# A Fourier mixer with a gated feed-forward net: the eight PSUM banks shared out anew between transforms and first layer

## The chip, the cores and the metric

One core of one Trainium2 chip runs the whole program. The metric is device time in microseconds (us) of one execution, the median of several runs. TensorE (PE in the profile; PEld is its weight load) does the matrix products into PSUM, which has eight banks of 512 fp32 columns on 128 partitions. ScalarE (ACT) and VectorE (DVE) read PSUM and free its banks; GpSimd (POOL) and SyncE (SP) issue most DMAs here.

## The reference

```python
X = np.fft.rfft(x, axis=1)                  # x: 8 x 3008 x 256
Yr = Xr @ w_r - Xi @ w_i + b_r
Yi = Xr @ w_i + Xi @ w_r + b_i
Y = soft_threshold(Yr, 0.01) + 1j * soft_threshold(Yi, 0.01)
y = np.fft.irfft(Y, n=3008, axis=1)         # then 24064 tokens of 256
gate = 1 / (1 + np.exp(-(y @ w_gate)))      # 256 -> 1536
out = (gate * (y @ w_val)) @ w_out          # 1536 -> 256
```

The feed-forward weights arrive as 64-bit floats and are turned on the chip into pairs of fp32r words (high and low part); a product of two such pairs is three matmuls.

## The kernel before

**The transform.** A sequence of 3008 = 47 x 64 is transformed in two steps. Step A of a sequence (`fwd_a`, eight units) multiplies by the 47-point table `fa_sb`; step B (`fwd_b`) does the 64-point part, `mix` (or `mix4` for the first sequence) multiplies by `w_r` and `w_i`, `inv_b` goes back by 64 points, and `inv_a` (units again) goes back by 47 points. Between the steps the data goes through HBM: `zd` after step A, `vd` after `inv_b`, and `yd` for the finished tokens that the last stage uses.

A unit of step A holds two row halves of an input tile (`j`, partitions 0 to 46 and 64 to 110) and two column groups (`c`). `products_a` takes two PSUM tiles `pa[0]` and `pa[1]`, one for each `j`, and issues four 47x64x512 fp32 products, which use four different quarters of the array; each is two records in the trace. Then the two banks are copied out, by ACT and DVE or by ACT alone (L191). `halves_a` does the same for the third and fourth sequences with tiles `xfh` loaded in halves and results in `azh` tiles of tag `st`, of which there are `NST` = 3; `inv_b` puts its result `vz` (L327) into the same tag.

**The banks.** Pool `psf` has `FFT_BANKS` = 3 banks, shared by all transform tiles: `pa` (2 for a unit), `pb` (1, freed by the copy `xsf`, L264), `pm` and `pm3` (2 for a mix, freed by DVE, L288 to L293), `pi` (1, freed by the copy `vz`), `pia` (2 for a unit of `inv_a`). Pool `psl` has `L1_BANKS` = 3 banks for the first layer (`pg` and `pv` of `ffn1`) and `L2_BANKS` = 2 for the second (`po` of `ffn2`). When the transforms are done, `psf` is closed and `psg` opened in its place.

**The stages.**
1. Sequence 0 and half of sequence 1 go through step A, then sequence 0 through B, mix and back. The first feed-forward weights are converted beside it (`ops`, `start_part`). The order is written by hand (`tc.manual_schedule`).
2. Twelve `ffn` units (token chunk 0, one for each of the 12 slices of 128 hidden columns), also by hand: `ffn1` for a slice, then `ffn2` for the slice two before, then one or two `halves_a` units. The conversion of the remaining weights is woven into `ffn1` by `hook`.
3. The other 96 `ffn` units, with the other sequences' transforms spread between them by weights (`rates`). Here the framework's planner orders the instructions of each engine: by the order of the program where its own model finds the operands and a free bank, otherwise something later goes first.
4. The remaining 19 pairs of 512-token blocks, without transforms: `half` forms seven products for each 2 x 2 block of the first layer in four banks (`open_banks`: `pa1`, `pb1`, `pc1` from `psl`, `pd1` from `psg`), with `second` between them, by hand.

In the page, L189 is the product of step A, L191 its copies, L251 `fwd_b`, L286 `mix`, L308 `mix4`, L323 to L325 `inv_b`, L359 `inv_a`, L423 to L425 `ffn1`, L429 the sigmoid that frees `pg`, L431 the multiplication that frees `pv`, L451 to L453 `ffn2`, L658 to L660 `second`, L683 the products of stage 4, L810 to L818 the conversion, L861 matmuls on zeros or weights that keep TensorE busy.

Of the kernel before, what the change touches and what calls it, by code (L numbers as in the profile page):

```python
# [9 lines left out]
F32 = mybir.dt.float32  # L10
# [9 lines left out]
R2, R1 = 47, 64  # L20
# [4 lines left out]
CW = 512  # L25
NPL = 9
HW = 512
FFT_BANKS, L1_BANKS, L2_BANKS = 3, 3, 2

NF2K, NR2K, NLD, NST, NBIG, NMF, NME, NVF, NVO, NHH, NSG, NYF = 5, 4, 3, 3, 5, 3, 2, 2, 1, 3, 2, 3  # L30
NCB, NTMP, NHP = 10, 9, 12


# [73 lines left out]
def tile_fft_mix_ffn(ctx: ExitStack, tc, x, w_r, w_i, b_r, b_i, w_one, w_out, mf, mi, mis, fa, fb, out):  # L107
    nc = tc.nc

    B, D, S = x.shape[0], w_r.shape[0], R1 * R2  # L110
    P = 128
# [19 lines left out]
    fft = ExitStack()  # L131
    cw = fft.enter_context(tc.tile_pool(name="cw", bufs=1))
    p2 = fft.enter_context(tc.tile_pool(name="p2", bufs=2))
    psl = ctx.enter_context(tc.tile_pool(name="psl", bufs=3, space=bass.MemoryType.PSUM))
    psfs = ExitStack()
    psf = psfs.enter_context(tc.tile_pool(name="psf", bufs=FFT_BANKS, space=bass.MemoryType.PSUM))

    def bank(name, tag="fft", bufs=FFT_BANKS):
        return (psf if tag == "fft" else psl).tile([P, 512], F32, tag=tag, bufs=bufs, name=name)
# [8 lines left out]
    fa_sb = cw.tile([P, P], F32, name="fa_sb")[:, :64]  # L148
# [32 lines left out]
        move(nc.sync, xf, xv[b, h])  # L181
        held["x", b, h] = xf

    def products_a(xs, outs, copies):
        pa = [bank("pa") for _ in range(2)]
        for j in range(2):
            rows = slice(64 * j, 64 * j + R2)
            for c in range(2):
                nc.tensor.matmul(pa[j][64 * c:64 * c + 64], fa_sb[rows], xs[c][rows], start=True, stop=True)  # L189
        for copy, o, t in zip(copies, outs, pa):  # L190
            copy(o, t.rearrange("p (h c) -> p h c", h=2))  # L191

    def fwd_a(b, h):

        xf = held["x", b, h]
        at = xf[:, 0:2], xf[:, 2:4]
        products_a(at, at, (nc.scalar.copy, nc.vector.tensor_copy if b < 2 else nc.scalar.copy))

    def store_a(b, h, queue=nc.sync):
        move(queue, held.pop(("x", b, h)), zv[b][h], True)  # L200
# [6 lines left out]
    def halves_a(b, u):  # L207

        xs = [held.pop(("xh", b, 2 * u + c)) for c in range(2)]
        az = [p2.tile([P, 2, D], F32, tag="st", bufs=NST, name="azh") for _ in range(2)]  # L210
        products_a(xs, az, (nc.scalar.copy, nc.scalar.copy))
        for j in range(2):
            move(nc.gpsimd, az[j], zv[b][u, :, :, 2 * j:2 * j + 2], True)
# [179 lines left out]
    outs = {}  # L393
# [70 lines left out]
    def fft_units(bs, ms):  # L464
# [5 lines left out]
        def step_a(i):  # L470
            if i == 0:
                for k in range(min(PRE, len(aa))):
                    load_a(*aa[k])
            if i + PRE < len(aa):
                load_a(*aa[i + PRE])
            fwd_a(*aa[i])
            store_a(*aa[i])
# [103 lines left out]
    xs = {}  # L581
# [90 lines left out]
    banks = {}  # L672
# [12 lines left out]
        return product  # L685

    def open_banks(k):
        banks[k] = [bank(t, "l1", L1_BANKS)[:, :HW] for t in ("pa1", "pb1", "pc1")] + [
            psg.tile([P, 512], F32, tag="l1d", bufs=1, name="pd1")[:, :HW]]

    def half(k, extra):

# [3 lines left out]
        if k not in banks:  # L696
            open_banks(k)
            early = False
        else:
            early = True  # L700
# [188 lines left out]
    with tc.manual_schedule():  # L889
# [3 lines left out]
        for h in range(na):  # L893
            fwd_a(0, h)
            store_a(0, h)
            if h in (1, 3, 4):
                load_a(1, {1: 1, 3: 2, 4: 3}[h])
            if h == 2:
                load_mix()
# [7 lines left out]
        for h in range(EARLY):  # L907
            fwd_a(1, h)
            if h == 1:
                wi_sb = mix_weights()  # L910
# [109 lines left out]
    for j in range(NF, len(ffn)):  # L1020
        c, f = divmod(j, NF)
# [4 lines left out]
        while side and (acc >= side[0][0] or j >= (part if len(side) > n_last else end) - 1):  # L1026
# [12 lines left out]
            if not side:  # L1039
                psfs.close()  # L1040
                psg = ctx.enter_context(tc.tile_pool(name="psg", bufs=1, space=bass.MemoryType.PSUM, reuse_waits="tile"))
# [15 lines left out]


    open_banks(0)
    first_product = products(0)  # L1060
    a, b, c, d = banks[0]
# [62 lines left out]
```

## Time and profile before

| | us |
|---|---|
| median of 3 runs | 2793.51 |
| lowest, highest | 2792.45, 2795.2 |
| the profiled execution | 2796.54 |
| its span | 2794.7 |
| TensorE busy in the span | 2764.7 (99%) |
| VectorE busy | 2041.3 (73%) |
| ScalarE busy | 1362.3 (49%) |
| GpSimd busy | 726.4 (26%) |

TensorE's busy time counts a matmul until its modelled end: the second layer's 512-column matmuls stand with 0.39 us each, while one starts 0.23 us after the other. So busy time hides short waits, and the starts of the matmuls show them. The granted clock of TensorE is 0.988 of full speed over the span: it is at half speed from 14 to 41 us and for a few microseconds at some later places. The DMA engines are busy 91% of the first 50 us and 86% of the next 50, between 35 and 78% in each further stretch of 50 us up to 1100 us, and little after that.

### The profile page before, as it was taken

How to read it: one execution, taken by the hardware profiler on the slowest of the kernel's cores; microseconds unless marked ns; L12 is line 12 of the kernel's file. 1: busy time of each engine (PE TensorE's matmuls, PEld its weight loads, DVE VectorE, ACT ScalarE, POOL GpSimd, SP SyncE). 2: the span in 40 equal slices, each digit the busy share in tenths (PEclk: the TensorE clock that was granted, in tenths of full speed). 3: DMA queues.
4: the chain of work that ended last, by engine and by line, in shares of the span. 5: the costliest groups of instructions: out<-in, count | busy, mean ns of one | idle time of the engine just before them, and what ended most of it. 6: DMA issues, size and time to landing. Idle time of an engine off the chain costs nothing.

```text
span 2794.7 us, 45032 instructions
## 1 busy us (share of the span) xinstructions
PE 2764.7 (99%) x17224; PEld 2268.0 (81%) x17224; DVE 2041.3 (73%) x3010; ACT 1362.3 (49%) x2372; POOL 726.4 (26%) x674
## 2 busy tenths in 40 slices
PE   8999999999999999999999999999999999999999
PEld 5658888878899878888888888888888888888887
DVE  4667777767677635877777777777777777777776
ACT  4565555555555534444444444444444444444443
POOL 0231001113300001333333333333333333333321
PEclk8999999999999999999999999999999999999999
DMA  9776645666655472000000000000000000000000
GB/s 268 226 236 186 183 143 157 177 196 200 193 143 146 142 219 81 16 15 31 31 31 16 16 31 31 16 16 31 31 30 16 16 31 31 16 16 31 31 16 15
DMA packets 170503, 241.43 MB, mean 86 GB/s; under 512 B 17328, under 2 KB 127536, under 8 KB 170288
## 3 DMA queue, kind: packets, MB, share of 16 engines
q1 hardware_dynamic: 159648, 214.92, 25.8%
q0 software_dynamic: 10496, 23.60, 2.7%
q8 instruction: 136, 2.23, 0.4%
q14 instruction: 79, 0.65, 0.1%
q10 hardware_dynamic: 144, 0.03, 0.0%
HBM read 134.15 MB, written 104.33 MB: 85 GB/s over the span
## 4 chain that ended last, share of the span: by engine, by line
PE 92%; DVE 3%; DMA 3%; ACT 2%; issue 1%; SPq 0%; ACTq 0%; POOL 0%; DVEq 0%; POOLq 0%
PE pd L683 11%; PE pa L683 11%; PE pc L683 11%; PE po L659 7%; PE po L660 7%; PE po L658 7%; PE pm L286 6%; PE pb L683 6%; PE pia L359 3%; PE pb L251 3%; PE pg L423 2%; PE pa L189 2%; PE po L451 2%; PE pg L424 2%; PE pg L425 2%; PE pv L424 2%
## 5 line engine op out<-in xcount | busy, mean ns | idle before, releaser
L658 PE MATMUL po<-hh,w 128*128 128x512 f32 x912 | 354.8, 389 | 0.0
L659 PE MATMUL po<-hh,w 128*128 128x512 f32 x912 | 354.8, 389 | 0.0
L660 PE MATMUL po<-hl,w 128*128 128x512 f32 x912 | 354.8, 389 | 0.0
L742 POOL TENSOR_TENSOR c<-c,c 128x512 f32<-128x512 f32 x114 | 147.2, 1292 | 792.1 <-DVE c L738 598.7
L683 PE MATMUL pc<-s,w1h 128*128 128x512 f32 x912 | 280.8, 389 | 0.0
L683 PE MATMUL pa<-a,w1h 128*128 128x512 f32 x912 | 280.8, 389 | 0.0
L738 DVE TENSOR_TENSOR c<-u,pc 128x512 f32<-128x512 f32 x228 | 156.5, 686 | 92.3 <-PE pc L683 86.3
L713 DVE TENSOR_TENSOR u<-u,pb 128x512 f32<-128x512 f32 x228 | 155.3, 681 | 90.0 <-PE pb L683 61.1
L630 ACT CAST hh<-v 128x512 fp32r<-128x512 f32 x114 | 70.7, 620 | 305.5 <-DVE v L723 305.5
L634 POOL TENSOR_TENSOR hl<-c,hh 128x512 fp32r<-128x512 f32 x114 | 152.5, 1337 | 186.0 <-ACT hh L630 186.0
L658 PEld LDWEIGHTS po<-hh,w 128*128 128x128 f32 x912 | 171.2, 188 | 35.6
L683 PEld LDWEIGHTS pc<-s,w1h 128*128 128x128 f32 x912 | 171.2, 188 | 35.6
L683 PEld LDWEIGHTS pa<-a,w1h 128*128 128x128 f32 x912 | 171.2, 188 | 35.6
L659 PEld LDWEIGHTS po<-hh,w 128*128 128x128 f32 x912 | 171.2, 188 | 35.5
L660 PEld LDWEIGHTS po<-hl,w 128*128 128x128 f32 x912 | 171.2, 188 | 35.5
L286 PE MATMUL pm<-w_sb,xsh 128*128 128x256 f32 x1008 | 189.8, 287 | 3.2 <-ACT xf L191 2.5
L683 PE MATMUL pa<-a,w1l 128*128 128x512 f32 x456 | 177.4, 389 | 0.0
L683 PE MATMUL pc<-s,w1l 128*128 128x512 f32 x456 | 177.4, 389 | 0.0
L715 DVE TENSOR_TENSOR v<-u,pc 128x512 f32<-128x512 f32 x228 | 156.7, 687 | 24.5 <-DVE u L713 0.5
L744 DVE TENSOR_TENSOR u<-u,pd 128x512 f32<-128x512 f32 x228 | 156.6, 687 | 24.5 <-DVE c L738 0.9
L717 DVE TENSOR_TENSOR v<-v,pd 128x512 f32<-128x512 f32 x228 | 156.7, 687 | 24.4 <-DVE v L715 0.9
L709 ACT COPY u<-pa 128x512 f32<-128x512 f32 x228 | 133.7, 586 | 70.1 <-PE pa L683 70.1
(175 smaller groups left out, 6672.9 us busy)
## 6 DMA issues: line engine op xcount, KB each, us to landing
zf<-zd SPq DMA_DIRECT2D x96, 256.0 KB, 3.1
vf<-vd SPq DMA_DIRECT2D x128, 192.0 KB, 3.7
out_dram<-ot SPq DMA_DIRECT2D x93, 256.0 KB, 2.2
vd<-vz SPq DMA_DIRECT2D x84, 256.0 KB, 2.9
ypair<-yd SPq DMA_DIRECT2D x19, 1024.0 KB, 4.9
yd<-yf SPq DMA_DIRECT2D x103, 188.0 KB, 3.5
xf<-in_x_dram SPq DMA_DIRECT2D x96, 192.0 KB, 4.4
zd<-xf SPq DMA_DIRECT2D x88, 192.0 KB, 2.9
```

The lines of the kernel that those rows point to most:

```text
L286: nc.tensor.matmul(o, l, r, start=(i == 0), stop=(i == len(mms) - 1))
L634: sub_(hl, h, hh)
L658: nc.tensor.matmul(o, wh, hh, start=(f == 0), stop=False)
L659: nc.tensor.matmul(o, wl, hh, start=False, stop=False)
L660: nc.tensor.matmul(o, wh, hl, start=False, stop=(f == NF - 1))
L683: nc.tensor.matmul(o, l, r, start=not more and l is wh and r is xh, stop=l is wl, skip_group_check=more)
L713: add(u, u, b)
L715: add(v, u, c)
L717: add(v, v, d)
L738: add(c12, u, c)
L742: nc.gpsimd.tensor_mul(c12, g12, c12)
L744: add(u, u, d)
```

## The change

The sizes: four banks for the transforms, two for the first layer, and four `st` tiles instead of three. A unit of step A gets one further product (three in `halves_a`) ahead of its four: it is two columns wide, goes to the bank and the row half (and, in `halves_a`, the column groups) that the first of the four does not touch, and its result is overwritten by the product proper. In the first sequence, units 2 and 5 take their two banks from the first layer's pool. In stage 4 `pc1` moves from `psl` to `psg`, beside `pd1`.

```diff
-FFT_BANKS, L1_BANKS, L2_BANKS = 3, 3, 2
+FFT_BANKS, L1_BANKS, L2_BANKS = 4, 2, 2
...
-    NST = 3        # in the list of sizes
+    NST = 4
...
-    psl = ctx.enter_context(tc.tile_pool(name="psl", bufs=3, space=bass.MemoryType.PSUM))
+    psl = ctx.enter_context(tc.tile_pool(name="psl", bufs=2, space=bass.MemoryType.PSUM))
...
-    def products_a(xs, outs, copies):
-        pa = [bank("pa") for _ in range(2)]
+    def products_a(xs, outs, copies, where=()):
+        pa = [bank("pa", *where) for _ in range(2)]
+        for j, c in ((1, 0),) if xs[0] is xs[1] else ((1, 0), (1, 1), (0, 1)):
+            rows = slice(64 * j, 64 * j + R2)
+            nc.tensor.matmul(pa[j][64 * c:64 * c + 64, :2], fa_sb[rows], xs[c][rows, c, :2], start=True, stop=True)
+        xs = [t[:, 2 * c:2 * c + 2] if t.shape[1] == 4 else t for c, t in enumerate(xs)]
...
-        at = xf[:, 0:2], xf[:, 2:4]
-        products_a(at, at, (nc.scalar.copy, nc.vector.tensor_copy if b < 2 else nc.scalar.copy))
+        products_a((xf, xf), (xf[:, 0:2], xf[:, 2:4]), (nc.scalar.copy, nc.vector.tensor_copy if b < 2 else nc.scalar.copy),
+                   ("l1", L1_BANKS) if b == 0 and h % 3 == 2 else ())
...
-        banks[k] = [bank(t, "l1", L1_BANKS)[:, :HW] for t in ("pa1", "pb1", "pc1")] + [
-            psg.tile([P, 512], F32, tag="l1d", bufs=1, name="pd1")[:, :HW]]
+        banks[k] = [bank(t, "l1", L1_BANKS)[:, :HW] for t in ("pa1", "pb1")] + [
+            psg.tile([P, 512], F32, tag="l1d", bufs=2, name=t)[:, :HW] for t in ("pc1", "pd1")]
```

More of the change, by code (lines that the diff above doesn't have):

```diff
@@ L27 @@
 HW = 512
-FFT_BANKS, L1_BANKS, L2_BANKS = 3, 3, 2
-NF2K, NR2K, NLD, NST, NBIG, NMF, NME, NVF, NVO, NHH, NSG, NYF = 5, 4, 3, 3, 5, 3, 2, 2, 1, 3, 2, 3
+FFT_BANKS, L1_BANKS, L2_BANKS = 4, 2, 2
+NF2K, NR2K, NLD, NST, NBIG, NMF, NME, NVF, NVO, NHH, NSG, NYF = 5, 4, 3, 4, 5, 3, 2, 2, 1, 3, 2, 3
 NCB, NTMP, NHP = 10, 9, 12
```

## The prediction

> **What bounds the kernel now.** I read the busy times by stage first (columns: stretch, its length, then busy us and instructions of PE, PEld, DVE, ACT and POOL, the granted clock, the DMA share, GB/s).
>
> ```profile
> core 0: us, PE busy (x) PEld busy (x) DVE busy (x) ACT busy (x) POOL busy (x), PEclk, DMA share, GB/s
> 0.00:40.24 40.24, 32.59 (x119) 12.51 (x120) 12.40 (x21) 10.46 (x17) 0.20 (x4) 0.68 0.92 255
> 40.24:112.30 72.06, 67.84 (x477) 57.02 (x475) 49.96 (x83) 46.55 (x87) 15.19 (x24) 0.95 0.84 253
> 112.30:202.30 90.00, 83.87 (x517) 51.60 (x517) 56.22 (x97) 53.50 (x97) 30.42 (x58) 0.88 0.78 236
> 202.30:965.00 762.70, 756.81 (x7060) 640.79 (x7058) 551.98 (x934) 436.13 (x740) 103.88 (x159) 1.00 0.58 169
> 965.00:1080.00 115.00, 112.77 (x1517) 90.15 (x1510) 34.52 (x50) 44.45 (x88) 5.52 (x4) 0.97 0.72 201
> 1080.00:2794.70 1714.70, 1710.85 (x7547) 1415.91 (x7545) 1336.25 (x1826) 771.19 (x1346) 571.18 (x426) 1.00 0.07 23
> ```
>
> PE bounds all but the first 202 us. The last stage (1715 us) keeps four banks and their order, so the change can act on the first 1080 us only. By PE's waits there seems to be little to win (us in total, times, longest):
>
> ```profile
> PE pa L189 <- ACT xf L191: 6.4, 11, 1.5
> PE pa L189 <- ACT azh L191: 4.3, 2, 2.3
> ```
>
> But a matmul counts as busy to its modelled end, which covers short waits. Start times show them. Here is a forward unit (L189) of each kind, the quick one first, then a slow one with what surrounds it:
>
> ```profile
> 307.68 1.09 PE L189 MATMUL pa<-xf,fa_sb 47*64 47x512 f32 x8
> ...
> 329.00 0.68 DVE L288 TENSOR_TENSOR yt<-pm,bias_sb 128x512 f32<-128x512 f32 x1
> ...
> 329.81 0.28 PE L325 MATMUL pi<-yh,mi_sb 128*128 128x256 f32 x1
> 330.02 1.82 PE L189 MATMUL pa<-xf,fa_sb 47*64 47x512 f32 x8
> 330.13 0.59 ACT L327 COPY vz<-pi 128x512 f32<-128x512 f32 x1
> ...
> 330.76 0.20 PEld L189 LDWEIGHTS pa<-xf,fa_sb 47*64 47x64 f32 x4 [0.55 <-ACT vz L327]
> ```
>
> The slow unit follows `inv_b`. With three banks its second `pa` gets the bank that `pi` has just filled; the copy `vz` ends at 330.72, and the second pair's weights load at 330.76. The two pairs, which otherwise run at once on different quarters of the array, run one after the other: 1.82 against 1.09 us, 0.73 lost with no idle PE shown. The inverse units (L359) have the same two speeds:
>
> ```profile
> 151.03 1.15 PE L359 MATMUL pia<-fb_sb,vf 48*64 48x47 f32 x64
> ...
> 347.64 1.88 PE L359 MATMUL pia<-fb_sb,vf 48*64 48x47 f32 x64
> ...
> 932.37 1.88 PE L359 MATMUL pia<-fb_sb,vf 48*64 48x47 f32 x64
> ```
>
> **1. Four banks in the planned stage (202 to 965 us).** The weight loads' waits there, and the busy time of L189 alone (202.30 to 760.00) and L359 alone (202.30 to 965.00), in the columns of the first table without the other engines:
>
> ```profile
> PEld pa L189 <- ACT vz L327: 10.0, 18, 0.6
> PEld pm L286 <- ACT xf L191: 3.5, 4, 1.5
> 202.30:760.00 557.70, 51.63 (x258) 10.77 (x256) 1.00 0.61 178
> 202.30:965.00 762.70, 65.84 (x2752) 59.99 (x2752) 1.00 0.58 169
> ```
>
> Forward: 18 units wait for `vz`, 18 x 0.73 = 13.1 us. All 32 units take 51.6 us where 32 x 1.09 = 34.9 would do, so 16.7 is the most there is. Inverse: 2752 / 64 = 43 units take 65.8 us against 43 x 1.15 = 49.5, at most 16.4; 15 of them, the first and the last shown above, have the full 1.88, so 15 x 0.73 = 11.0. With a fourth bank a step's `pb`, `pm`, `pm3`, `pi` no longer take one of their own back: the unit behind gets the banks of `pb` and of `pm`, and DVE has read `pm` by 329.68, before the unit starts at 330.02. What is late next is that DVE read, 0.3 us ahead of need. I take the 24.1 us that name `vz`, half of the other 9.0 (4.5), and 2 of the 3.5 us in which `pm` waited for a unit's copies: 30.6. Ends: 0, if the planner keeps the pairs apart for another reason, and 16.7 + 16.4 + 3.5 = 36.6. DVE is busy 552 of 763 us there and ACT 436, so 31 us less leaves PE the bound.
>
> **2. The two-column products.** They bring no transfer and no wait that the unit's own products lack; they move the wait for the second bank and the second half's load ahead of the first pair, which is then queued behind it. Where both are ready, only PE time is added. Nearest row, 47 columns wide:
>
> ```profile
> L359 PE MATMUL pia<-fb_sb,vf 48*64 48x47 f32 x4096 | 97.7, 235 | 5.7 <-DMA vf<-vd 3.9 <-ACT xf L191 0.8 <-issue 0.7
> ```
>
> In the quick unit at 151.03 a record takes 1.15 / 64 = 18 ns of the stream; one alone lasts 235 ns. A product is two records: 0.036 us, or 0.47 if nothing overlaps. In the planned stage that is 32 x 0.036 = 1.2 us (at most 15.0); the stage is a dense stream like the first row, so 1.2. Ahead of 202 us PE is not the bound, and its waits cover the other 16 units' products and the 48 of `halves_a`. TensorEngine Tiling (Array Packing) of the Trainium skill, section Instruction Overhead, gives each matmul about 60 cycles however narrow it is; at 2.4 GHz I estimate 25 ns a record from it, so 1.6 us instead of 1.2, and the measured 18 ns, four quarters at once, is lower.
>
> **3. Stage 2 (112 to 202 us).** Here the conversion sets the pace: DVE and ACT hand a chain of small operations to each other, and one turn, from L810 to the next L810, takes 5.80 us.
>
> ```profile
> 138.73 2.91 PE L189 MATMUL pa<-xfh,fa_sb 47*64 47x512 f32 x12
> 139.58 0.42 DVE L810 TENSOR_SCALAR cv_e<-raw 128x512 uint32<-128x512 uint32 x1
> 143.95 1.97 PE L189 MATMUL pa<-xfh,fa_sb 47*64 47x512 f32 x4 [2.31 <-ACT azh L191]
> 145.19 1.21 ACT L191 COPY azh<-pa 128x512 f32<-128x512 f32 x2 [1.29 <-DMA zd<-azh]
> 145.38 0.42 DVE L810 TENSOR_SCALAR cv_e<-raw 128x512 uint32<-128x512 uint32 x1
> 148.56 0.58 ACT L191 COPY azh<-pa 128x512 f32<-128x512 f32 x1 [2.17 <-DMA zd<-azh]
> ...
> 178.27 0.58 ACT L191 COPY azh<-pa 128x512 f32<-128x512 f32 x1 [2.07 <-DMA zd<-azh]
> ```
>
> Where two half units stand together, PE lacks a bank (2.31 us) and ACT lacks an `st` tile, whose store is still under way; the rest of the conversion queues behind that copy. `NST` 4 holds both units' results, four banks both units' products. ACT's waits lie in the chain: 1.29 + 2.17 + 2.07 = 5.5 us, which I take. PE's wait lies beside it. Ends: 0, if weights or inputs come no sooner (the DMA share is 0.78), and 5.5 + 2.31 + about as much at the second such place = 10.
>
> **4. Opening, banks of the first layer.** Six banks remove the wait between units (0.52 us), but PE does not set the pace:
>
> ```profile
> 17.13 2.12 PE L189 MATMUL pa<-xf,fa_sb 47*64 47x512 f32 x8 [0.52 <-ACT xf L191]
> 32.70 0.92 SPq L243 DMA_DIRECT2D zf<-zd  x2
> 35.81 4.63 PE L861 MATMUL warm<-zero 128*128 128x512 f32 x10
> 40.24 2.53 PE L251 MATMUL pb<-mf_sb,zf 128*128 128x128 f32 x16
> zf<-zd SPq DMA_DIRECT2D x8, 256.0 KB, 4.7
> ```
>
> DMA is busy 0.92 of the time to 40.24, and the load of `zf` (32.70) follows stores that queue in it. It lands at about 32.70 + 4.7 = 37.4, while L251 starts at 40.24, behind the forward units of sequence 1 and ten warming matmuls. If these end earlier, L251 can start up to 2.8 us sooner; I take 2.5, which leaves 0.3 for what still ends late. Least: 0, if the inputs of sequence 1 land no sooner.
>
> **5. Two first-layer banks.** `pg` now waits for the sigmoid of the slice before, `pv` for its multiplication; behind them in PE's queue stand `ffn2` and the transforms.
>
> ```profile
> 134.41 0.50 PE L423 MATMUL pg<-yth,w1h 128*128 128x512 f32 x1
> 135.07 0.58 ACT L429 ACTIVATE sg<-pg 128x512 f32<-128x512 f32 x1
> ...
> 1071.55 0.60 ACT L429 ACTIVATE sg<-pg 128x512 f32<-128x512 f32 x1 [0.68 <-PE pg L425]
> 1074.07 0.39 PE L423 MATMUL pg<-yth,w1h 128*128 128x512 f32 x1
> ```
>
> In stage 2 a sigmoid ends at 135.65, 1.24 us after the next `pg` has started; there the conversion chain sets the pace and covers it. At 1071.55, with no transform between, the sigmoid ends 1.9 us ahead of the next `pg`, and with transforms between, more. Cost 0; upper end 5, four such waits. `pc1` in `psg` keeps one bank a product: 0.
>
> **Sum.** 30.6 - 1.2 + 5.5 + 2.5 = 37.4 us off the profiled 2796.5 (span 2794.7): 2759.1. That execution lies 3.0 above the median of 2793.5, so the prediction is 2756. All upper ends give 36.6 + 10 + 2.8 = 49 off the median: 2744.
>
> **Rivals.** *The pairs stay apart in half the units* (22 in 100): the planner orders by its own model, and the second bank is late by its reckoning or by DVE's read of `pm`. For it: 0.3 us of slack. Against: the first pair now must have that bank (`pm3`'s is read later, `pb`'s went to `pi`), and it starts 0.21 us behind the last `pi` matmul. It gives half of 30.6, so 2793.5 - 15.3 - 5.5 - 2.5 + 1.2 = 2771. The leading products do not help then: TensorE: Matmul & The Clock Gate of the Trainium skill (part 3, The mechanism) says that matmuls start and end in strict order, and the row at 330.02 agrees, its second pair 0.74 us behind.
>
> *Nothing comes of it* (7): the four banks are filled and emptied at the same DVE and ACT pace, so waits move to `pm`, and full-latency products (15.0) eat the rest: 2793.5 - 15.3 + 15.0 = 2793. DVE's 72% in the stage speaks against.
>
> *Slower* (8): with two banks `pg` hangs on ACT, whose queue holds transform copies ahead of the sigmoid. If the 1.24 us of 134.41 were lost at half of the 107 turns, 66 us would go: 2756 + 66 = 2822. It decides from 0.35 us a turn (37.4 / 107). Against: the 1.9 us at 1071.55, in the tightest run of `ffn` units.
>
> **How the numbers follow.** The remaining 63 in 100 are the forecast, 2742 to 2766 by itself. The range reaches up over the half case to 2780 and leaves out some 17 in 100. What can be told from no change is 0.2%, 5.6 us: faster 0.85, the two first cases; same 0.07; slower 0.08.
>
> **What would show it.** Right: units of L189 and L359 behind L325 at about 1.1 us, no PEld wait of L189 for `vz`, no ACT wait for `zd<-azh` between 140 and 180, L251 first at about 38, and the last stage as long as now. Wrong: L189 units still at 1.8, PEld waits of `pg` for the sigmoid, or DVE reads of `pm` (L288) that release L189.

## The result, and the profile after

The changed kernel takes 2751.12 us in the median (2746.54 to 2753.95), the kernel before, run beside it, 2794.36 (2792.45 to 2798.92): a ratio of 0.9841, 95% interval 0.9821 to 0.9862. The profiled execution of the changed kernel took 2746.54 us, at the low end of its runs, that of the kernel before 2796.54. So the two traces lie 50 us apart and the medians 43. One of five runs of the changed kernel in a later batch took 2850.96 us at a granted clock of 0.894; the ratios and intervals leave it out.

The first view is again the busy time by stage (stretch, its length, busy us and instructions of PE, PEld, DVE, ACT and POOL, granted clock, DMA share, GB/s), of the changed kernel, cut at places that match the prediction's table (the second cut stands 1.0 us behind the first inverse product of stage 2 in both, the third at the first `pg` of slice 12).

```profile
0.00:37.39 37.39, 30.34 (x144) 13.43 (x145) 12.40 (x21) 10.56 (x17) 0.20 (x4) 0.68 0.92 245
37.39:111.33 73.94, 64.59 (x491) 55.96 (x489) 50.19 (x83) 46.87 (x87) 15.20 (x24) 0.94 0.86 261
111.33:188.07 76.74, 72.93 (x595) 47.84 (x595) 54.53 (x95) 50.91 (x93) 30.60 (x56) 0.97 0.87 267
188.07:918.07 730.00, 727.15 (x7140) 623.75 (x7136) 551.92 (x937) 434.48 (x744) 105.70 (x160) 1.00 0.61 177
918.07:1029.99 111.92, 110.68 (x1509) 88.78 (x1509) 34.23 (x50) 44.34 (x88) 5.51 (x4) 0.98 0.74 207
1029.99:2744.80 1714.81, 1710.88 (x7547) 1416.34 (x7545) 1336.32 (x1826) 771.42 (x1346) 571.13 (x426) 1.00 0.07 23
```

Against the table of before, the planned stage is 32.7 us shorter (762.70 to 730.00) and stage 2 13.3 (90.00 to 76.74). The opening loses 2.9 us up to the first L255 (it was L251; most lines have moved by four) and gives 1.9 back in the row behind it. The stretch ahead of the last stage is 3.1 shorter, and the last stage is as long as it was. DVE and ACT are busy as long in the planned stage as before (552 us, and 434 against 436), and PE has no product less: what has gone is the time that its products stood behind one another.

How it went is seen in a forward unit behind `inv_b`, the case that was slow before (timeline of the changed kernel, start, duration, engine, line, operation):

```profile
313.76 0.42 DVE L296 TENSOR_TENSOR ys<-pm,yt 64x256 f32<-64x256 f32 x1
313.77 0.28 PE L329 MATMUL pi<-yh,mi_sb 128*128 128x256 f32 x1
...
313.98 0.21 PE L188 MATMUL pa<-xf,fa_sb 47*64 47x2 f32 x1
...
313.98 0.66 PE L193 MATMUL pa<-xf,fa_sb 47*64 47x512 f32 x3
...
314.05 0.19 PE L188 MATMUL pa<-xf,fa_sb 47*64 47x2 f32 x1
314.08 0.59 ACT L331 COPY vz<-pi 128x512 f32<-128x512 f32 x1
314.11 1.05 PE L193 MATMUL pa<-xf,fa_sb 47*64 47x512 f32 x5
...
315.09 0.50 PE L427 MATMUL pg<-yth,w1h 128*128 128x512 f32 x1
```

The copy `vz` still runs from 314.08 to 314.67, and DVE still reads a bank of the mix at 313.76 (`pm3`: the profile leaves the number out), but the unit has neither of these banks. No weight load of the unit waits for them: both pairs are under way by 314.11, and PE goes on to `pg` at 315.09, 1.11 us behind the unit's start. In the planned stage's list of PEld waits of before, `vz` stood with 10.0 us; in the changed kernel's it releases no `pa` and no `pia`, and the largest row of `pa` and that of `pm` are these (188 to 919 us; us in total, times, longest):

```profile
PEld pa L188 <- issue: 3.0, 9, 0.4
PEld pm L290 <- ACT xf L195: 0.8, 2, 0.6
```

Counted from a unit's start to the next instruction's start, 18 of the 33 forward groups of the planned stage took 1.8 us before and one does now; of the inverse groups 23 of 44 took 1.1 us and 17 took 1.8 or 1.9, now 40 of 43 take 1.0 or 1.1. (A group is one unit, part of one, or several with nothing between.)

In stage 2 the conversion now keeps its pace in most turns (ACT's timeline, changed kernel):

```profile
138.14 0.59 ACT L433 ACTIVATE sg<-pg 128x512 f32<-128x512 f32 x1
139.46 0.69 ACT L818 ACTIVATE raw<-raw 128x512 f32<-128x512 uint32 x1 [0.73 <-DVE raw L817]
140.06 0.62 ACT L443 CAST hh<-sg 128x512 fp32r<-128x512 f32 x1
140.59 2.04 ACT L195 COPY azh<-pa 128x512 f32<-128x512 f32 x4
142.77 0.67 ACT L821 CAST w<-raw 128x512 fp32r<-128x512 f32 x1
143.35 0.72 ACT L815 ACTIVATE cv_e<-cv_e,ebias 128x512 int32<-128x512 int32 x1
143.97 0.57 ACT L433 ACTIVATE sg<-pg 128x512 f32<-128x512 f32 x1
```

From sigmoid to sigmoid this turn takes 5.83 us. All four copies of the two half units that stand together run in one go (140.59 to 142.63), where the prediction's rows of before have ACT waiting 1.29 and 2.17 us for `st` tiles and PE 2.31 for a bank; the same turn took 9.34 us there. Three of the changed kernel's eleven turns from sigmoid to sigmoid are still longer (6.20, 7.69 and 7.04 us), and two are shorter (5.25 and 5.17).

### The profile page after: what moved, and what is told of

Its sections match the earlier page's. It is cut to its first block, busy times and chain, and to the rows that moved or that the text cites. A ratio compares the mean times of both kernels' runs of the same rounds, so it can differ in the third digit from the quotient of the medians.

```text
span 2744.8 us, 45406 instructions
## 1 busy us (share of the span) xinstructions
PE 2716.6 (99%) x17416; PEld 2246.1 (82%) x17416; DVE 2039.6 (74%) x3010; ACT 1358.6 (49%) x2372; POOL 728.3 (27%) x674
## 4 chain that ended last, share of the span: by engine, by line
PE 92%; DVE 3%; DMA 3%; ACT 1%; issue 1%; SPq 0%; DVEq 0%; ACTq 0%; POOLq 0%
PE pd L687 11%; PE pc L687 11%; PE pa L687 11%; PE po L664 8%; PE po L662 8%; PE po L663 8%; PE pm L290 6%; PE pb L687 6%; PE pb L255 3%; PE pia L363 2%; PE pg L427 2%; PE po L455 2%; PE pg L428 2%; PE pg L429 2%; PE po L456 2%; PE pv L428 2%
## 5 line engine op out<-in xcount | busy, mean ns | idle before, releaser
L634 ACT CAST hh<-v 128x512 fp32r<-128x512 f32 x114 | 70.7, 620 | 305.7 <-DVE v L727 305.7
```

## The experiments

Stage 2 is measured here from the first product of `pg` to that of slice 12 (83.0 us before, 70.2 in the changed kernel's first trace), stage 3 from there to the last product of `pm` (757.9 and 725.2). Each kernel was timed beside the kernel before, whose medians there were 2792.5 to 2794.9; stages are from one trace of each kernel.

**The banks alone.** The changed kernel without the leading products, without the first layer's banks in the opening, and with `NST` 3.

```diff
-        for j, c in ((1, 0),) if xs[0] is xs[1] else ((1, 0), (1, 1), (0, 1)):
-            ... (the leading product)
-    NST = 4
+    NST = 3
-                   ("l1", L1_BANKS) if b == 0 and h % 3 == 2 else ())
+                   ())
```

> The shares of the banks alone (4 transform, 2 first layer, pc1 beside pd1): no leading products, three st tiles, the opening's units all in the transforms' banks. Bank theory: a unit behind inv_b runs its pairs at once because its second bank is no longer the one inv_b has just filled, so stage 3 (first pg of slice 12 to the last pm) is as short as in the changed kernel (725.2 us against 757.9) or some 3 us shorter, since 32 leading products of 0.10 us are gone; stage 2 lies between 83 and 70 us; in all 2750 to 2758 us. Rival, that the leading products do it by taking the waits ahead of the unit: units of step A stay at 1.75 us and stage 3 is about 742 us long, 2770 us or more in all.

2755.99 us, ratio 0.9863 (0.9844 to 0.9882). Stage 3 takes 721.4 us, 36.5 less than before; stage 2 80.6, 2.5 less. All three are what the bank theory expected. Busy time of the forward products (L190) and of the inverse ones (L360) in stage 3:

```profile
200.12:760.00 559.88, 36.67 (x260) 7.01 (x256) 1.00 0.64 187
200.12:926.00 725.88, 49.90 (x2752) 44.51 (x2752) 1.00 0.60 178
```

Against 51.63 and 65.84 before, 15.0 and 15.9 us have gone: the banks alone bring the pairs together, nearly all of them, with no leading product.

**Without the leading products.**

```diff
-        for j, c in ((1, 0),) if xs[0] is xs[1] else ((1, 0), (1, 1), (0, 1)):
-            rows = slice(64 * j, 64 * j + R2)
-            nc.tensor.matmul(pa[j][64 * c:64 * c + 64, :2], ...)
```

> The changed kernel without the leading products. Bank theory: they only cost, 0.10 us (1.12 against 1.02 from start to next start) in each of 32 units of stage 3, so 2745 to 2750 us where the changed kernel has 2751, units of step A at 1.02 us. Rival, that the planner keeps the two pairs together only because of them: units at 1.75 us again, 32 x 0.7 less the cost, 2765 to 2770 us.

2748.4 us, 0.984 (0.9822 to 0.9858): the times do not tell it from the changed kernel. Stage 3 takes 721.2 us, 3.9 less than with them, and the units of step A take 1.02 us, so the rival is out.

**With three staging tiles.**

```diff
-    NST = 4
+    NST = 3
```

> The changed kernel with three st tiles. Staging theory: where two half units stand together ACT waits again for the store of an azh tile, 1.3, 2.2 and 2.1 us in the conversion's chain, so stage 2 is 5 to 6 us longer than the changed kernel's 70.2 us and the whole 2756 to 2757 us. Rival, that PE's missing bank and the half clock behind it made stage 2 long: stage 2 stays within 1.5 us of 70.2, 2751 us.

2760.48 us, 0.9875 (0.9857 to 0.9894). Stage 2 takes 76.2 us, 6.0 more, as the staging theory has it, and stage 3 725.5; the median lies some 4 us above what it expected. ACT waits for stores again, in stage 2:

```profile
ACT azh L195 <- DMA zd<-azh: 7.0, 4, 2.8
```

The granted clock was 1.00 from 122 us to the stage's end here, so of these 6 us at most what the first turn has more (6.09 against 5.25) can be the half clock's.

**The fourth staging tile alone**, put into the kernel before.

```diff
-    NST = 3
+    NST = 4
```

> The kernel before with a fourth st tile alone (3 transform banks, 3 first-layer banks, no leading products). Staging theory: the st tile is worth about 6 us of stage 2 by itself, because ACT's wait for a store lies in the conversion's chain whatever PE does: stage 2 (first pg of slice 0 to first pg of slice 12) 77 us instead of 83.0, stage 3 unchanged at 757.9, 2787 us. Rival, that the fourth tile is of use only with four banks, since with three the second of two half units is late anyway at PE: stage 2 stays above 80 us, 2792 us.

2791.92 us, 0.9995 (0.9982 to 1.0008); stage 2 82.1. My expectation for it missed and the rival's held. Its waits tell why. First the kernel with four banks and three tiles (the banks alone), then this one with three banks and four tiles, both in stage 2:

```profile
ACT azh L192 <- DMA zd<-azh: 10.3, 5, 4.9
```

```profile
PE pa L189 <- ACT azh L191: 5.4, 2, 3.3
```

With the banks alone the products are ready, and ACT stands 10.3 us for `st` tiles whose stores are under way. With the tile alone, PE stands up to 3.3 us for a bank, and the copies come late for that. Neither alone gives more than 2.5 us of the 12.8. The kernel with three tiles above, which has the four banks and the leading products, stands between (76.2 us). The granted clock of stage 2 was 0.90 before and with the tile alone, 0.92 with the banks alone and 1.00 in the changed kernel; how much of the stage's length hangs on it, beside the tile and the banks, is not separated.

**The leading products alone**, put into the kernel before.

```diff
+        for j, c in ((1, 0),) if xs[0] is xs[1] else ((1, 0), (1, 1), (0, 1)):
+            ... (the leading product)
```

> The kernel before with the leading products alone (3 transform banks, 3 first-layer banks, three st tiles). Bank theory: units behind inv_b still wait for the copy vz, now ahead of all four products, and last 1.75 to 1.9 us; nothing gained, 2794 to 2800 us. Rival, that the leading products bring the gain: units at 1.1 us, 2775 us or less.

2791.88 us, 0.9993 (0.9982 to 1.0004), 2 us under what I expected; stage 3 761.4 us, 3.5 more than before. The units still wait for the copy, and 18 of them take 1.8 us (stage 3). In the unit at 331.69 the wait stands ahead of three of the four products, not of all four:

```profile
PEld pa L193 <- ACT vz L330: 8.0, 18, 0.5
```

Stage 2 takes 78.7 us, 4.3 less than before, which I did not expect; point 2 below comes back to it.

**Two banks for the first layer, the freed one unused.**

```diff
-FFT_BANKS, L1_BANKS, L2_BANKS = 3, 3, 2
+FFT_BANKS, L1_BANKS, L2_BANKS = 3, 2, 2
...
+            psg.tile([P, 512], F32, tag="l1d", bufs=2, name=t)[:, :HW] for t in ("pc1", "pd1")]
```

> The kernel before with the first layer's pool cut to two banks and nothing else in stages 1 to 3 (3 transform banks, one bank unused; stage 4 with pc1 beside pd1; three st tiles, no leading products). Theory that the third first-layer bank is idle cover: pg waits for the sigmoid a few times in stage 2 (about 5 us of PE idle, beside the conversion's chain), nowhere else, stages 3 and 4 as long as before, 2793 us, at most 2 us more. Rival, that two banks tie PE to ACT's queue: stage 3 longer by more than 5 us, 2798 us or more.

2793.6 us, 1.0001 (0.9989 to 1.0013). Stage 2 takes 81.3 us and stage 3 755.7, neither longer than before. In stage 2 weight loads of `pg` wait three times for the sigmoid, 4.0 us in all, and PE stands idle for 1.4 of the 5 us expected; in stage 3 none waits for it. The third bank was not needed.

**The opening without the first layer's banks.**

```diff
-                   ("l1", L1_BANKS) if b == 0 and h % 3 == 2 else ())
+                   ())
```

> The changed kernel without the first layer's banks in the opening: all units of sequence 0 use the four transform banks. DMA theory: the opening is set by the loads and stores, and four banks are as good as six, so L255 starts within 0.7 us of 37.4 and the whole is 2751 us. Rival, that the six banks bring the opening's gain: L255 starts at 39 us or later, 2753 to 2754 us.

2748.47 us, 0.9834 (0.9814 to 0.9854). L255 starts at 37.27, where PE has waited 1.20 us for the load of `zf`, as the DMA theory has it. Here are the last products ahead of it in this kernel, then in the changed one (PE's timeline):

```profile
32.64 3.43 PE L865 MATMUL warm<-zero 128*128 128x512 f32 x10
37.27 0.91 PE L255 MATMUL pb<-mf_sb,zf 128*128 128x128 f32 x6 [1.20 <-DMA zf<-zd]
```

```profile
31.00 2.03 PE L193 MATMUL pa<-xf,fa_sb 47*64 47x512 f32 x8
32.95 4.63 PE L865 MATMUL warm<-zero 128*128 128x512 f32 x10
37.39 0.88 PE L255 MATMUL pb<-mf_sb,zf 128*128 128x128 f32 x5
```

The warming matmuls began at 35.81 before and begin at 32.6 to 33.0 now, with the first layer's banks or without.

**Leading products in the halves only.**

```diff
-        for j, c in ((1, 0),) if xs[0] is xs[1] else ((1, 0), (1, 1), (0, 1)):
+        for j, c in () if xs[0] is xs[1] else ((1, 0), (1, 1), (0, 1)):
```

> The changed kernel with leading products in the half units of stage 2 only, none in the forward units. If the leading products cost 0.10 us in each of 32 units of stage 3 and are worth about 1 us in stage 2, this is 3 to 4 us faster than the changed kernel in stage 3 (721.3 against 725.2) with the same stage 2 (70.2): 2747 us. Rival, that what runs without them in stage 2 and 3 differs only by chance: within 1 us of 2751.

2749.09 us, 0.9844 (0.9823 to 0.9866). Stage 3 takes 722.9 us, 2.3 less than the changed kernel and close to the kernels without any. Stage 2 takes 74.8, not the 70.2 expected: ACT waits 3.9 us for stores of `azh` (1.2 in the changed kernel), and one turn lasts 8.64 us (7.04 there). The edit leaves the half units as they are, and why the stores were late is open.

**A longer conversion chain.**

```diff
-            "mant": lambda: v.tensor_single_scalar(high, high, 0xFFFFF, op=ALU.bitwise_and),
+            "mant": lambda: [v.tensor_single_scalar(high, high, 0xFFFFF, op=ALU.bitwise_and) for _ in range(2)],
```

> The changed kernel with one operation of the 16-bit conversion (the mask that takes the mantissa, 0.43 us on VectorE in its row) done twice, which leaves its value as it is: the turn of the chain grows by one such operation. Theory: with four banks, stage 2 (first slice of pg to the thirteenth, 70.2 us) stands on that chain, twelve turns of 5.80 us. Then each turn reads 6.2 us and stage 2 some 5 us more, 75 us, and the median some 2755. Rival: TensorE sets stage 2 and the chain only happens to be near; then stage 2 stays within 1 us of 70.2 and the median within 2 us of the changed kernel's.

2753.45 us, 0.9853 (0.984 to 0.9866). Stage 2 takes 74.4 us. That alone would not decide, as the 74.8 above shows, nor does the median; the single turns do. Two sigmoids of this kernel:

```profile
162.80 0.59 ACT L433 ACTIVATE sg<-pg 128x512 f32<-128x512 f32 x1
...
169.08 0.58 ACT L433 ACTIVATE sg<-pg 128x512 f32<-128x512 f32 x1
```

and the two of the changed kernel that answer to them:

```profile
157.47 0.58 ACT L433 ACTIVATE sg<-pg 128x512 f32<-128x512 f32 x1
...
163.28 0.58 ACT L433 ACTIVATE sg<-pg 128x512 f32<-128x512 f32 x1
```

6.28 us against 5.81. The undisturbed turns read 6.27 to 6.30 here and 5.80 to 5.86 in the changed kernel: the doubled operation's time (the two take 0.90 where one takes 0.43) shows in full in each of these turns. So the chain sets the pace of stage 2 wherever a turn is undisturbed; with its longer turns the stage grows by 4.2 us, not by the 5.6 of twelve turns.

**The changed kernel without leading products and without the first layer's banks in the opening, and the changed kernel again beside it.**

> The four transform banks, the two first-layer banks and the fourth staging tile, without the leading products and without the first-layer banks in the opening. Theory: both things left out bring nothing, so stage 3 takes 721 us as in the other kernels without leading products, stage 2 some 71, and the median is 2747, some 2 to 4 us under the changed kernel. Rival: the leading product covers waits that stage 2 has in some units; then stage 2 is 2 us or more longer than 71 and the two medians are equal.

> The changed kernel as it is, again, beside the other two on one chip. Its median should lie within 3 us of 2751, and its stretches within 1 us (stages 3 and 4) and 3 us (opening, stage 2) of those in its first trace; what differs by more is what one trace can't tell.

The plain one: 2745.21 us (2744.01 to 2748.07), 0.9828 (0.9815 to 0.9842). The changed kernel again: 2751.3, 0.9845 (0.9831 to 0.9858). The intervals overlap, so the 6 us between the medians are not shown as a whole, though all four runs of the plain kernel lie below all of the other's on the same chip (from 2748.56). What the traces show is stage 3: 722.6 us against 725.9. The forward unit that answers to the one at 313.98, in the plain kernel:

```profile
315.31 1.09 PE L190 MATMUL pa<-xf,fa_sb 47*64 47x512 f32 x8
316.32 0.50 PE L424 MATMUL pg<-yth,w1h 128*128 128x512 f32 x1
```

1.01 us to the next product, against 1.11 with the leading one. Stage 2 takes 72.4 us in the plain kernel and 70.7 in the repeated one, L255 starts at 36.38 and 37.39, and the first `pg` at 118.75 and 119.01.

## Why the prediction was right, point by point

The time of 2751 lies 5 us below the 2756 predicted, inside the range and inside the forecast's own 2742 to 2766. Not every term has its size.

**1. Four banks: mechanism right, size too low.** For the predicted 30.6 us, 32.7 came with the leading products in the way, and 36.5 with the banks alone: the upper end of 36.6. The units came down by 15.0 and 15.9 us (of 16.7 and 16.4), and the waits of `pm` for a unit's copies from 3.5 to 0.8. So the half that I took of the 9.0 us beyond the 24.1 was mis-sized: 6.8 came instead of 4.5. Another 0.7 came from `pm`, and 2.9 of the 36.5 stand in no row shown here. One reading was wrong: only the 13.1 us of the forward units name `vz`. For the inverse units the list of waits names it once, with 0.4 us; I had counted them by their 1.88 us. That they came down with the fourth bank shows that the bank was the cause there too. DVE's read of `pm`, named as late next, releases no `pa` in the planned stage of the changed kernel, and one (0.8 us) in that of the plain one. The planner kept the pairs together, so the rival of half the units did not come about. That rival took the order of starts for strict. The records of the unit at 313.98 do not bear that out: three products start between the two records of the leading product (313.98 and 314.05). In which order they were issued the trace does not show.

**2. Leading products: too cheap by three.** I took 0.036 us for one, from the rate of a dense stream. It costs 0.10 (1.11 against 1.01): 3.2 us for 32 units, and 3.3 to 4.1 in stage 3 by the four pairs of kernels with and without it. The rows at 313.98 show the place. Three of the four products start there at once, while the fourth, whose quarter of the array the leading product occupies, starts at 314.11, behind its two records; the unit ends with that quarter. In the plain kernel all eight records stand in one row from 315.31. So what counts is not the share of a stream but how long two records, one behind the other, hold one quarter: 0.13 us. TensorEngine Tiling (Array Packing) of the Trainium skill, section Instruction Overhead, from which I had estimated 25 ns a record (1.6 us in all), is nearer than my 18 ns and still half of what was measured; the measurement decides. The medians do not tell 3 us here, and so the kernels with and without come out alike. A gain from the leading products is not shown in any stretch, but in stage 2 it is not ruled out. With four `st` tiles that stage differs by 2 us at most in their favour (70.2, 70.7 and 71.2 against 71.0 and 72.4). With three tiles it differs by more: 78.7 against 83.0 in the kernel before, and 76.2 against 80.6 with four banks, where the first layer's banks in the opening differ too. Without a cause in the edit it varied by as much (74.8 in the kernel with leading products in the halves), and these are single traces.

**3. Stage 2: too low by 7.** I added up the three waits of ACT that I saw, 5.5 us. In stretches that begin and end alike it was 12.8 (83.0 to 70.2). The list of ACT's waits of before (110 to 202 us) has a second row, which the sum left out:

```profile
ACT azh L191 <- DMA zd<-azh: 5.5, 3, 2.2
ACT azh L191 <- PE pa L189: 3.1, 4, 1.1
```

Four times ACT waited for products that PE had formed late; in the changed kernel (110 to 190 us) this row is gone, and the first has one wait of 1.2 us left, at 173.35. That is a small miss of the sign which said there would be none between 140 and 180. What went from the two rows makes 7.4 of the 12.8 us. Nearer than any sum of waits is the length of the stage when none is left: a turn takes 5.80 us, and twelve make 69.6. Only six of the changed kernel's eleven turns lie within 0.03 of that, though, and the longer and shorter ones cancel, so that it fits 70.2 so closely is in part chance. The two changes do it together: banks alone 2.5, tile alone 1.0, both 10.6 and 12.0 without leading products (72.4 and 71.0).

**4. Opening: right at its place, lost behind it, and from another cause.** L255 starts 2.85 us sooner (2.5 predicted). But the four banks of `psf` do it, since the kernel without the loan from the first layer starts it at 37.27, and the kernels with three banks at 39.2 to 40.3. And it does not last: the first `pg` starts at 117.9 and 119.0 in two executions of the changed kernel, at 119.3 before, and between 116.4 and 121.2 in all others. The term should have been 0.3 to 1.4, which is within that spread.

**5. Two first-layer banks: 0, as predicted.** The wait that I named as a sign against me is there, in stage 2 of the changed kernel:

```profile
PEld pg L427 <- ACT sg L433: 7.2, 6, 1.6
```

It costs nothing, because the conversion covers it: the kernel with two banks and nothing else is no slower, and the doubled conversion operation lengthens each undisturbed turn by its full time. In the planned stage no weight load of `pg` waits for it. So the slower rival had its wait, but where PE does not set the pace.

**What stays open.** The 3.1 us between the last `pm` and the last stage are not explained: that stretch took 116 to 121 us in all kernels, with no order by what they change. Executions of the changed kernel spread over 7 us around the median, and no trace shows why.

The terms erred in both directions: some 6 and 7 us too little in the first and third, 2 to 3 too much in the second and 1 to 2 in the fourth. Against the profiled execution, by which they were sized, the sum is 12.6 us short (37.4 of 50.0), 3.1 of that in the unexplained stretch. That it lies only 5 us off the median is in part luck: errors of opposite sign cancel, and the profiled execution of the changed kernel was a quick one, so that the medians lie 7 us less apart than the two traces by which the terms are judged.

## What to carry to other kernels

When two products that should run together take turns, look at which buffer the second one was handed: in a rotating pool it can be the one that the product just ahead has filled, and the engine's idle time does not show it, starts do. For a stage that a chain paces, multiply the undisturbed turn by the number of turns as a second estimate: here it came nearer than adding the waits that one had picked out. And undo one part at a time: here one part carried stage 3, two did most of stage 2, together, and of two no gain could be shown.

## What the runs showed of the hardware that was not expected

A product of two columns ahead of a packed group of four holds its quarter of the array for 0.13 us and makes the group 0.10 us longer, where records in a dense stream of narrow products follow each other at 0.018 us. And one PSUM bank less made no difference that shows in one place (1.0001, 0.9989 to 1.0013, with a bank left unused), while one more took 36.5 us off stage 3 in another.
